# Pooled attention and two expert layers on one core: the maximum of the scores is subtracted by TensorE in PSUM, and ScalarE copies the router logits

## The chip, the cores and the metric

The kernel runs on one core of a Trainium2 chip. The metric is the device time of one execution in microseconds; lower is better. TensorE has two clock levels, 1.2 and 2.4 GHz, and the profile shows the granted share of the full clock for every stretch.

## The reference, cut to what matters

Three stages follow one another. Keys and values are averaged over groups of eight rows, so that each of the 576 queries of a head sees 72 pooled keys. The softmax subtracts the row maximum before the exponential. Two expert layers (router, then the product with the chosen expert's weights) come after it.

```python
k_p = k.reshape(B, H, Sp, pool, D).mean(axis=3)
v_p = v.reshape(B, H, Sp, pool, D).mean(axis=3)
scores = scale * np.matmul(q, k_p.transpose(0, 1, 3, 2))
scores = scores - np.max(scores, axis=-1, keepdims=True)
attn = np.exp(scores)
attn = attn / (np.sum(attn, axis=-1, keepdims=True) + 1e-09)
return np.matmul(attn, v_p)          # then _moe_ref and _moe2_ref
```

B = H = 8, S = 576, D = 64, pool = 8, so Sp = 72.

## The kernel before

The attention works through 36 chunks `c` of 128 tokens, all eight heads at once. Each chunk is a chain over four engines, and the chain is spread over several turns of one loop, so that every engine has work of several chunks in its queue. Every engine executes its queue in the order in which the code was written.

In one turn of the loop, for chunk `c`, these steps are issued:

- `emit_S(c)`: TensorE multiplies the transposed queries `qt` with the pooled keys `KB` into `ps_s` (two banks of PSUM; there is one such buffer, so the next chunk's product waits until the last reader is done). Inside it stands `emit_qT(c + 2)`, four transposes of queries and their copy `qt` by ScalarE. VectorE reduces `ps_s` to the eight maxima `mx`, then subtracts them into `ec` in SBUF; ScalarE takes the exponential of `ec` in place.
- `emit_eT(c - 1)`: TensorE transposes the exponentials of the chunk before into `ps_et`, ScalarE copies them to `et`.
- `emit_AV(c - 3)`: TensorE multiplies `et` with `VB` (pooled values, a column of ones and the values times the router's weights) into `ps_av`. VectorE makes `rec` (two operations), `lg` and the attention output `x` out of it. The rest of that chunk, the sum `ls`, the logits `LG` and the copy of the logits into the last eight columns of `x`, is issued in the next turn, around the maximum and the subtraction of chunk `c + 1`.
- `prep_...` and `pool_...`: the sums over eight rows (on GpSimd, and a third of the values on VectorE, the instruction `v<-v` of line 172) and their transposes and copies for later batches. `VB<-v,half` and `VB<-ps_g,half` are VectorE's part of the values' preparation.
- `bg.tick()`: one small step of a background chain (routing of finished tokens), at fixed places between these.

Of every nine chunks one holds the last 64 tokens of two batches; its products are done in two halves of 64 rows. I call it a mixed chunk. The first block of the first expert layer starts between the last chunks (`moe.gemm1_early`), and everything after the attention follows from there, mostly at the pace of TensorE.

The lines that the change and the prediction's steps touch are these, with the numbers of the profile: 293 (product of the scores), 303 (`mx`), 307 (subtraction), 309 (exponential), 327 and 329 (`et`), 347 (product with the values), 366 to 382 (what VectorE does with it), 172, 247 and 259 (pooling and preparation on VectorE).

Of the kernel before, what the change touches and what calls it, by code (L numbers as in the profile page):

```python
# [19 lines left out]
POOL = 8  # L20
# [14 lines left out]
# Tiles of pooled rows of K: four, from the third batch on.  # L35
# [3 lines left out]
# Pooled rows (head, sp) of one batch: five tiles for K, six chunks for V.  # L39
# [4 lines left out]
def segments(t):  # L44
    """Pieces of a tile of pooled rows that belong to one batch: (b, sp0, sp1, first partition)."""
    g0, end = TILES[t]
    g = g0
    while g < end:
        b, sp = divmod(g, SP)
        n = min(SP - sp, end - g)  # L50
        yield b, sp, sp + n, g - g0
        g += n


def attention(tc, g, q, k, v, mid, w_gate, bias, const, moe):
    """Pooled attention; rows of (x, router logits) go to g.xd in token order, logits to g.LG.

    The first block of the first layer starts while the last tokens are still at work."""
    nc = tc.nc
    with ExitStack() as ctx:  # L60
# [46 lines left out]
        def load_kb(b, i0, i1):  # L107
            """Pooled rows (head, sp) of K of one batch, tiles i0 to i1."""
            if ("kb", b) not in raw_t:
                raw_t["kb", b] = raw.tile([128, 5, POOL * D], F32, tag="k", name="kb", bufs=3)  # L110
            a = raw_t["kb", b]
            n = KR[i0][1] - KR[i0][0]
            nc.sync.dma_start(out=a[0:n, i0:i1, :],
                              in_=rows(k, b, KR[i0][0], KR[i1 - 1][1], i1 - i0))
# [53 lines left out]
        def pool_rows(out, a, eng):  # L168
            """Sums over the rows of a pool: a [n, m, POOL * D] to out [n, m, D]."""
            n, m = a.shape[0], a.shape[1]  # L170
            if eng is nc.vector:
                eng.tensor_reduce(out=out, in_=a.rearrange("p h (r d) -> p h d r", r=POOL),
                                  axis=AX.X, op=ALU.add)
            else:
                t1 = tree.tile([128, 4, 4 * D], F32, tag="t1", name="t1")[0:n, 0:m]
                t2 = tree.tile([128, 4, 2 * D], F32, tag="t2", name="t2")[0:n, 0:m]
                eng.tensor_tensor(t1, a[:, :, 0:4 * D], a[:, :, 4 * D:], ALU.add)
                eng.tensor_tensor(t2, t1[:, :, 0:2 * D], t1[:, :, 2 * D:], ALU.add)
                eng.tensor_tensor(out, t2[:, :, 0:D], t2[:, :, D:], ALU.add)
# [19 lines left out]
        def prep_kb(b, eng=None):  # L199
            """Even heads to the upper half of the partitions, odd ones to the lower."""  # L200
# [9 lines left out]
            # the last head in the place of the first, which the lower half doesn't need  # L210
# [77 lines left out]
        def emit_S(c, then=lambda: None):  # L288
            t = qT.pop(c)
            ps = ps_s.tile([128, 2, 512], F32, tag="s", name="ps_s")  # L290
            for b, p0, p1 in parts(c):
                for hp in range(4):
                    nc.tensor.matmul(ps[p0:p1, hp // 2, (hp % 2) * 144:(hp % 2) * 144 + 144],
                                     lhsT=t[:, hp, p0:p1], rhs=KB[b % NR][:, hp, :],
                                     start=True, stop=True)
# [3 lines left out]
            mx = sm.tile([128, 2, 4], F32, tag="mx", name="mx")  # L299
            ec = ep.tile([128, 2, 4, SP], F32, tag="ec", name="ec", bufs=2)  # L300
            e = ec.rearrange("p g h s -> p (g h s)")
# [5 lines left out]
            nc.vector.tensor_tensor(ec, view, mx.unsqueeze(3).to_broadcast([128, 2, 4, SP]),  # L307
                                    ALU.subtract)
            nc.scalar.activation(out=e, in_=e, func=ACTF.Exp, scale=1.0 / (POOL * 8.0))
            bg.tick()  # L310
# [3 lines left out]
            e_t[c] = e  # L314
# [43 lines left out]
        def after_AV(c, ps):  # L358
# [23 lines left out]
            V.tensor_copy(x[:, r, DM:XW], g.LG[:, c, :])  # L382
# [41 lines left out]
        # loads in the order of their use  # L424
# [27 lines left out]
        # the part of a chunk's rows that belongs to its first and to its second head  # L452
# [10 lines left out]
        # the clock of the tensor engine rises while nothing has come yet  # L463
# [10 lines left out]
        emit_S(0, lambda: emit_qT(1))  # L474
        for j in range(6):
            h = 4 * (j // 3) + j % 3
            i = 64 * (j % 2)
            nc.scalar.copy(WGV[i:i + 64, j // 2, j % 2].rearrange("p (a e) -> p a e", a=2),
                           wg[i:i + 64, h:h + 2, :])
        pool_v(0, 0, nc.vector)  # L480

        def bias_table():
            """The bias of every token: (1 - m) * b0 + m * b1."""
# [40 lines left out]
        for c in range(NC + LAG):  # L524
# [8 lines left out]
            elif c < 4:  # L533
                if c > 0:
                    emit_S(c)
                    emit_eT(c - 1)
                emit_qT(c + 2)
            elif c == NC - 1:
                emit_S(c, moe.gemm1_early)
            if 4 <= c < NC:  # L540
                emit_eT(c - 1)
            if c == NC - 1:
# [73 lines left out]
class Late:  # L616
    """The pool of the time of use."""
# [5 lines left out]
class Background:  # L623
    """Chains of small steps, spread between the steps of the main work."""
# [18 lines left out]
    def settle(self):  # L643
        """Until no product of theirs waits to be read."""
# [8 lines left out]
def setup(tc, g, const):  # L653
# [4 lines left out]
                            pattern=[[-1, 128]], channel_multiplier=1)  # L658
    g.LG = const.tile([128, C1, E], F32, name="LG")
# [12 lines left out]
def setup_routing(tc, g, const):  # L672
    """Constants and tables of both layers' routing."""
# [9 lines left out]
    # -1 where the row isn't before the column  # L683
# [49 lines left out]
    # the token of every column and partition, plus one, in two parts  # L733
# [44 lines left out]
def route(tc, g, r, lg, mask, c0, n, sp, pp, eng, wait=1, then=()):  # L778
    """The expert of every token of n columns, and its place among the expert's tokens, in steps."""
# [103 lines left out]
def together(*gens):  # L883
    """Steps of several chains in turn."""
# [10 lines left out]
def early_pick(tc, g, r, sp, pp, wait=4, fill=None):  # L895
    """The expert with the most tokens so far: its tokens come first."""
# [33 lines left out]
def keep_places(tc, g, r, n, f, sp):  # L930
    """Where fewer than n tokens of the first expert are known, the places up to n stay empty."""
# [14 lines left out]
def early_places(tc, g, r, C, j0, n, sp):  # L946
    """Which of the first C columns' tokens have one of n columns of places from j0 on."""
# [17 lines left out]
def early_slots(tc, g, r, C, gidx, sp, pp, empty=None):  # L965
    """The tokens of these places."""
# [33 lines left out]
def route_counts(tc, g, r, sp, pp, wait=1):  # L1000
    """Blocks of every expert; those of the first expert come first."""
# [33 lines left out]
def route_blocks(tc, g, r, sp):  # L1035
    """Every block's expert, and whether it isn't that of the block before."""
# [12 lines left out]
    # the tokens up to the end of a block's expert, less 256 for every block before  # L1049
# [26 lines left out]
def route_slots(tc, g, r, sp, pp, pace=1):  # L1076
    """The token of every slot."""
# [41 lines left out]
class Moe:  # L1119
    """The two expert layers, in blocks of T tokens of one expert."""  # L1120
# [91 lines left out]
    def zero(self):  # L1212
        """Nothing has a place in these columns before the eighteenth block."""
# [147 lines left out]
    def run(self):  # L1361
# [6 lines left out]
        # layer 1  # L1368
# [28 lines left out]
        # layer 2  # L1397
# [3 lines left out]
    def start2(self):  # L1401
        """Layer 2's first expert, and the tokens of its first two blocks, from 16 blocks of layer 1."""
# [13 lines left out]
    def gather_next(self, i):  # L1416
        """Block 0 of layer 2 in the place of block i of layer 1, if that doesn't exist."""
# [5 lines left out]
    def first2(self, n):  # L1423
        """Block 0 of layer 2, after n blocks of layer 1."""
# [36 lines left out]
    def deferred1(self, i, eng):  # L1461
        """Layer 2's gates of block i of layer 1, in steps."""
# [76 lines left out]
class Layer:  # L1539
    """Blocks of one layer, each prepared while the one before is computed."""  # L1540
# [22 lines left out]
    def second(self):  # L1563
        """Block 1, of the same expert as block 0; the places of the later ones are still at work."""
# [185 lines left out]
```

## Time and profile before

| | |
|---|---|
| time, median of 3 runs | 1028.99 us (1028.85 to 1032.23) |
| span of the profiled execution, first to last instruction | 1021.7 us |
| what lies around the span, against the median | 7.3 us |
| TensorE matmuls busy | 953.3 us (93%) |
| VectorE busy | 713.9 us (70%) |
| ScalarE busy | 526.0 us (51%) |
| GpSimd busy | 606.4 us (59%) |

The shares are means over the span. The attention is its first fifth (the maxima of the 36 chunks lie between 12.5 and 204.4 us), and the shares of that stretch are others than those of the expert layers, so they are read from the stretch. Engines are named PE (TensorE's matmuls), PEld (its weight loads), DVE (VectorE), ACT (ScalarE), POOL (GpSimd) and SP. An operation's row gives its start, its duration and, in brackets, how long its engine was idle before it and what ended the idle time.

### The profile page before, as it was taken

Reading aid. Unit: us, or ns where it says so; the run is one execution under the profiler, and the core shown is the slowest. Engines: PE = TensorE matmul, PEld = TensorE weight load, DVE = VectorE, ACT = ScalarE, POOL = GpSimd, SP = SyncE. Lnnn points to the kernel's source line nnn. Section 1 sums busy time; section 2 is a strip of 40 time slices with the busy share of each in tenths; the row PEclk is TensorE's granted clock in tenths of the full one; section 3 lists DMA queues with packets and bytes.
Section 4 is the critical chain, followed back from the end, with each engine's and each line's share of the span. In section 5 each row is a group of like instructions: output and inputs, shape, how many; then the busy total and the mean of one; then the engine's idle time right before and its main releaser. Section 6 shows DMA issues by size and latency. Waiting matters only on the chain. (4 is left out here: it accounts for less than half of the span.)

```text
span 1021.7 us, 20008 instructions
## 1 busy us (share of the span) xinstructions
PE 953.3 (93%) x6647; PEld 859.1 (84%) x6647; DVE 713.9 (70%) x1683; ACT 526.0 (51%) x1072; POOL 606.4 (59%) x816
## 2 busy tenths in 40 slices
PE   6888879899999999999999999999898999999995
PEld 5787879787788888888888888888786998888995
DVE  6699998886666666666666766667455667667665
ACT  4345545432455555555555655555313556555454
POOL 4675856554577777677777777767544333444442
PEclk8789989998999999999999999999899999999998
DMA  9998864520111111342223511226214662661341
GB/s 226 205 248 245 199 172 156 177 68 9 43 53 68 56 60 57 126 148 69 71 73 118 170 68 62 70 71 206 93 56 132 217 226 83 204 207 33 103 154 31
DMA packets 88353, 123.51 MB, mean 121 GB/s; under 512 B 15615, under 2 KB 52479, under 8 KB 88224
## 3 DMA queue, kind: packets, MB, share of 16 engines
q1 hardware_dynamic: 77904, 94.38, 30.9%
q0 software_dynamic: 10320, 27.59, 8.6%
q8 instruction: 59, 0.97, 0.4%
q14 instruction: 70, 0.57, 0.2%
HBM read 181.29 MB, written 39.48 MB: 216 GB/s over the span
## 5 line engine op out<-in xcount | busy, mean ns | idle before, releaser
L1300 PE MATMUL ps_g<-xh,w1h 128*128 128x256 f32 x992 | 289.2, 291 | 13.2 <-DVE hl L1304 8.0
L1300 PE MATMUL ps_g<-xl,w1h 128*128 128x256 f32 x992 | 280.2, 283 | 0.0
L1300 PE MATMUL ps_g<-xh,w1l 128*128 128x256 f32 x992 | 280.2, 282 | 0.0
L1253 POOL TENSOR_TENSOR w1l<-w1r,w1h 128x512 fp32r<-128x512 f32 x122 | 156.6, 1305 | 150.9 <-ACT w1h L1252 150.1
L1303 ACT ACTIVATE hh<-ps_g 128x256 fp32r<-128x256 f32 x248 | 95.5, 385 | 231.4 <-PE ps_g L1300 225.8
L1300 PEld LDWEIGHTS ps_g<-xh,w1h 128*128 128x128 f32 x992 | 188.2, 190 | 22.1 <-DVE hl L1304 10.5
L1314 PE MATMUL ps_g<-w2h,hh 128*128 128x512 f32 x464 | 190.5, 411 | 0.6 <-DVE rs_v L994 0.5
L1300 PEld LDWEIGHTS ps_g<-xl,w1h 128*128 128x128 f32 x992 | 188.6, 190 | 0.6 <-DVE xl L1269 0.2
L1300 PEld LDWEIGHTS ps_g<-xh,w1l 128*128 128x128 f32 x992 | 188.2, 190 | 0.0
L1314 PE MATMUL ps_g<-w2h,hl 128*128 128x512 f32 x464 | 185.1, 399 | 0.0
L1314 PE MATMUL ps_g<-w2l,hh 128*128 128x512 f32 x464 | 185.0, 399 | 0.0
L1259 DVE TENSOR_TENSOR w2l<-w2r,w2h 128x512 fp32r<-128x512 f32 x227 | 162.9, 719 | 17.7 <-ACT w2h L1258 1.5
L1304 DVE SCALAR_TENSOR_TENSOR hl<-ps_g,hh 128x256 fp32r<-128x256 f32 x248 | 105.0, 423 | 91.4 <-ACT hh L1303 85.9
L1258 ACT CAST w2h<-w2r 128x512 fp32r<-128x512 f32 x232 | 141.8, 612 | 3.0 <-DVE gidxf L997 3.0
L1252 ACT CAST w1h<-w1r 128x512 fp32r<-128x512 f32 x240 | 135.4, 618 | 4.9 <-DMA w1r<-in_moe_w_dram 4.9
L859 POOL TENSOR_SCALAR OB<-iota,BB,pay 128x128 bf16<-128x128 bf16 x126 | 110.8, 888 | 24.7 <-DVE BB L847 24.7
L1314 PEld LDWEIGHTS ps_g<-w2h,hl 128*128 128x128 f32 x464 | 88.3, 190 | 20.8
L1253 DVE TENSOR_TENSOR w1l<-w1r,w1h 128x512 fp32r<-128x512 f32 x118 | 101.2, 880 | 5.6 <-POOL rt_eq L796 5.2
L1314 PEld LDWEIGHTS ps_g<-w2h,hh 128*128 128x128 f32 x464 | 88.5, 191 | 18.1 <-issue 1.5
L1314 PEld LDWEIGHTS ps_g<-w2l,hh 128*128 128x128 f32 x464 | 88.6, 191 | 16.8
L1269 DVE TENSOR_TENSOR xl<-ps_x,xh 128x512 fp32r<-128x512 f32 x64 | 43.8, 686 | 57.3 <-ACT xh L1268 57.3
L1373 ACT ACTIVATE x<-ps_g,gate 128x512 f32<-128x512 f32 x37 | 25.5, 689 | 82.4 <-PE R L831 43.4
(256 smaller groups left out, 1463.9 us busy)
## 6 DMA issues: line engine op xcount, KB each, us to landing
w1r<-in_moe_w_dram SPq DMA_DIRECT2D x128, 512.0 KB
w2r<-in_moe_w_dram SPq DMA_DIRECT2D x128, 512.0 KB
x2s<-x SPq DMA_DIRECT2D x19, 522.0 KB
v<-in_v_dram SPq DMA_DIRECT2D x16, 576.0 KB
xd<-x SPq DMA_DIRECT2D x16, 520.0 KB
q_sb<-in_q_dram SPq DMA_DIRECT2D x16, 512.0 KB
kt<-in_k_dram SPq DMA_DIRECT2D x8, 576.0 KB
x2s<-OBx SPq DMA_DIRECT2D x16, 261.0 KB
```

Source lines behind the costliest of these rows:

```text
L859: e.tensor_scalar(g.ob(c)[:, i, :], g.iota, r.BB[:, c:c + 1], r.pay[:, i, c:c + 1], ALU.is_equal, ALU.mult)
L1252: self.nc.scalar.copy(self.w1h[f], raw)
L1253: (eng or self.nc.vector).tensor_tensor(self.w1l[f], raw, self.w1h[f].bitcast(F32), ALU.subtract)
L1258: self.nc.scalar.copy(self.w2h[f], raw)
L1259: (eng or self.nc.vector).tensor_tensor(self.w2l[f], raw, self.w2h[f].bitcast(F32), ALU.subtract)
L1269: nc.vector.tensor_tensor(self.xl[i % 2][:, :, 128 * t:128 * t + 128], ps, hi.bitcast(F32), ALU.subtract)
L1300: nc.tensor.matmul(ps, lhsT=a[f][:, k, :], rhs=b[:, k, :], start=(n == 0), stop=(n == 11))
L1303: nc.scalar.activation(out=self.hh[f], in_=ps, func=ACTF.Relu)
L1304: nc.vector.scalar_tensor_tensor(self.hl[f], in0=ps, scalar=0.0, in1=self.hh[f].bitcast(F32), op0=ALU.max, op1=ALU.subtract)
L1314: nc.tensor.matmul(ps, lhsT=a[f][:, tt], rhs=b[f], start=(n == 0), stop=(n == 23))
L1373: nc.scalar.activation(out=self.x2[i % 2][:, t, 0:DM], in_=ps, func=ACTF.Copy, scale=self.gate[i % 2][:, t:t + 1])
```

## The change

The subtraction leaves VectorE. VectorE writes the maxima `mx` in a type that TensorE reads in one pass (`F32R`, rounded). TensorE then adds minus the identity times `mx`, each maximum repeated over the 72 keys of its head, onto the scores where they lie in PSUM: two matmuls of 288 columns for each chunk. ScalarE takes the exponential straight from PSUM and writes `ec`. These two steps are a new function, `emit_exp(c)`, called after `emit_eT(c - 1)`. The product of the scores changes its start and stop flags, so that the later matmuls add to it. The copy of the logits into `x` goes from VectorE to ScalarE. Minus the identity, `nident`, is made once by GpSimd.

```diff
                     nc.tensor.matmul(ps[p0:p1, hp // 2, (hp % 2) * 144:(hp % 2) * 144 + 144],
                                      lhsT=t[:, hp, p0:p1], rhs=KB[b % NR][:, hp, :],
-                                     start=True, stop=True)
+                                     start=(hp % 2 == 0), stop=(hp % 2 == 1),
+                                     skip_group_check=True)
...
-            mx = sm.tile([128, 2, 4], F32, tag="mx", name="mx")
-            ec = ep.tile([128, 2, 4, SP], F32, tag="ec", name="ec", bufs=2)
-            e = ec.rearrange("p g h s -> p (g h s)")
+            mx = sm.tile([128, 2, 4], F32R, tag="mx", name="mx")
             next(av)
             nc.vector.tensor_reduce(out=mx, in_=view, axis=AX.X, op=ALU.max)
             bg.tick()
             next(av)
             bg.tick()
-            nc.vector.tensor_tensor(ec, view, mx.unsqueeze(3).to_broadcast([128, 2, 4, SP]),
-                                    ALU.subtract)
-            nc.scalar.activation(out=e, in_=e, func=ACTF.Exp, scale=1.0 / (POOL * 8.0))
-            bg.tick()
+            s_t[c] = ps, mx
             for _ in av:
                 pass
             bg.tick()
-            e_t[c] = e
+
+        s_t = {}
+
+        def emit_exp(c):
+            ps, mx = s_t.pop(c)
+            for gg in range(2):
+                nc.tensor.matmul(ps[:, gg, 0:288], lhsT=g.nident,
+                                 rhs=mx[:, gg, :].unsqueeze(2).to_broadcast([128, 4, SP]),
+                                 start=False, stop=True, skip_group_check=True)
+            e = e_t[c] = ep.tile([128, 8 * SP], F32, tag="ec", name="ec", bufs=2)
+            nc.scalar.activation(out=e.rearrange("p (g n) -> p g n", g=2), in_=ps[:, :, 0:288],
+                                 func=ACTF.Exp, scale=1.0 / (POOL * 8.0))
+            bg.tick()
...
-            V.tensor_copy(x[:, r, DM:XW], g.LG[:, c, :])
+            nc.scalar.copy(x[:, r, DM:XW], g.LG[:, c, :])
...
             if 4 <= c < NC:
                 emit_eT(c - 1)
+                emit_exp(c)
...
+    g.nident = const.tile([128, 128], F32R, name="nident")
+    nc.gpsimd.tensor_scalar(g.nident, g.ident, -1.0, None, ALU.mult)
```

The order of the queues shows where the new work stands. TensorE's queue before, one chunk without preparation and the start of the next (`ps_s` is the scores, `ps_q` the transposed queries, `ps_et` the transposed exponentials, `ps_av` the product with the values, three chunks back):

```order
L293 MATMUL ps_s<-KB_126,qt 128x144 x4
L272 MATMUL ps_q<-ident,qs 128x128 x4
L327 MATMUL ps_et<-ident,ec 96x128 x6
L347 MATMUL ps_av<-VB_132,et 128x146 x6
L293 MATMUL ps_s<-KB_127,qt 128x144 x4
```

The same place of the changed kernel:

```order
L293 MATMUL ps_s<-KB_128,qt 128x144 x4
L272 MATMUL ps_q<-ident,qs 128x128 x4
L336 MATMUL ps_et<-ident,ec 96x128 x6
L317 MATMUL ps_s<-mx,nident 128x288 x2
L356 MATMUL ps_av<-VB_134,et 128x146 x6
L293 MATMUL ps_s<-KB_129,qt 128x144 x4
```

The two new matmuls, which read the maxima `mx` of this chunk, stand ahead of the product with the values.

VectorE's queue before, from the maximum of one chunk to that of the next (`rec`, `lg` and `x` read the product with the values, `v<-v` is the pooling of values):

```order
L303 TENSOR_REDUCE mx<-ps_s 128x8
L380 TENSOR_TENSOR LG<-ls,BT 128x8
L307 TENSOR_TENSOR ec<-ps_s,mx 128x576
L382 COPY x<-LG 128x8
L366 TENSOR_SCALAR rec<-ps_av 128x8
L368 RECIPROCAL rec<-rec 128x8
L371 TENSOR_TENSOR lg<-ps_av,rec 128x64
L373 TENSOR_TENSOR x<-ps_av,rec 128x512
L172 TENSOR_REDUCE v<-v 96x64
L378 TENSOR_REDUCE ls<-lg 128x8
L303 TENSOR_REDUCE mx<-ps_s 128x8
```

The same stretch of the changed kernel:

```order
L302 TENSOR_REDUCE mx<-ps_s 128x8
L389 TENSOR_TENSOR LG<-ls,BT 128x8
L375 TENSOR_SCALAR rec<-ps_av 128x8
L377 RECIPROCAL rec<-rec 128x8
L380 TENSOR_TENSOR lg<-ps_av,rec 128x64
L382 TENSOR_TENSOR x<-ps_av,rec 128x512
L172 TENSOR_REDUCE v<-v 96x64
L387 TENSOR_REDUCE ls<-lg 128x8
L302 TENSOR_REDUCE mx<-ps_s 128x8
```

The subtraction and the copy are gone from between `LG` and `rec`; the rest stands as it stood.

ScalarE's queue before, one chunk (`qt` and `qs` are queries of later chunks, `vt` is a part of the values' preparation):

```order
L276 COPY qt<-ps_q 128x512
L309 ACTIVATE ec<-ec 128x576
L329 COPY et<-ps_et 96x768
L163 COPY qs<-q_sb 128x1024
L246 COPY vt<-ps_v 128x288
```

The same of the changed kernel:

```order
L276 COPY qt<-ps_q 128x512
L391 COPY x<-LG 128x8
L338 COPY et<-ps_et 96x768
L321 ACTIVATE ec<-ps_s 128x576
L163 COPY qs<-q_sb 128x1024
L246 COPY vt<-ps_v 128x288
```

The copy of the logits stands ahead of the copy `et`, and the exponential of this chunk has moved behind that copy.

## Rows read from the trace of the kernel before

**Rows 1.** The page: span and busy time of each engine.

```profile
span 1021.7 us, 20008 instructions
...
PE 953.3 (93%) x6647; PEld 859.1 (84%) x6647; DVE 713.9 (70%) x1683; ACT 526.0 (51%) x1072; POOL 606.4 (59%) x816
```

**Rows 2.** Busy time of each engine in two stretches of 20 us: PE, PEld, DVE, ACT and POOL, each with its count; then the granted clock, the DMA share and GB/s.

```profile
100.00:120.00 20.00, 19.26 (x162) 18.35 (x160) 19.68 (x52) 11.81 (x21) 13.90 (x15) 1.00 0.64 168
...
160.00:180.00 20.00, 20.00 (x200) 19.59 (x199) 15.35 (x47) 12.96 (x20) 9.34 (x11) 1.00 0.59 183
```

**Rows 3.** Groups of instructions by line in the first 260 us, shapes kept apart: count, busy us, mean ns of one, idle time of the engine before them and what ended it.

```profile
L329 ACT COPY et<-ps_et 96x768 f32<-96x768 f32 x36 | 28.0, 778 | 1.9 <-PE ps_et L327 1.9
L307 DVE TENSOR_TENSOR ec<-ps_s,mx 128x576 f32<-128x576 f32 x36 | 27.1, 753 | 0.7
...
L309 ACT ACTIVATE ec<-ec 128x576 f32<-128x576 f32 x36 | 24.6, 684 | 72.6 <-DVE ec L307 69.9 <-DVE x L382 2.6
...
L380 DVE TENSOR_TENSOR LG<-ls,BT 128x8 f32<-128x8 f32 x36 | 16.6, 462 | 0.1
...
L382 DVE COPY x<-LG 128x8 f32<-128x8 f32 x36 | 13.7, 380 | 0.1
...
L478 ACT COPY WGV<-wg 64x16 f32<-64x16 f32 x6 | 1.2, 203 | 1.6 <-DMA wg<-in_moe_w_gate_dram 1.6
```

**Rows 4.** VectorE in order of time, from the maximum of chunk 7 to that of chunk 8: start, duration, instruction.

```profile
57.87 0.74 DVE L303 TENSOR_REDUCE mx<-ps_s 128x8 f32<-128x576 f32 x1
58.53 0.15 DVE L380 TENSOR_TENSOR LG<-ls,BT 128x8 f32<-128x8 f32 x1
58.71 0.76 DVE L307 TENSOR_TENSOR ec<-ps_s,mx 128x576 f32<-128x576 f32 x1
59.38 0.16 DVE L382 COPY x<-LG 128x8 f32<-128x8 f32 x1
59.45 0.16 DVE L366 TENSOR_SCALAR rec<-ps_av 128x8 f32<-128x8 f32 x1
...
60.63 1.06 DVE L172 TENSOR_REDUCE v<-v 96x64 f32<-96x512 f32 x1
61.61 0.26 DVE L378 TENSOR_REDUCE ls<-lg 128x8 f32<-128x64 f32 x1
61.78 0.75 DVE L303 TENSOR_REDUCE mx<-ps_s 128x8 f32<-128x576 f32 x1
```

**Rows 5.** All engines in order of time around the end of chunk 12's subtraction: what TensorE starts when it is done.

```profile
86.54 0.75 DVE L307 TENSOR_TENSOR ec<-ps_s,mx 128x576 f32<-128x576 f32 x1
...
87.40 1.03 PEld L293 LDWEIGHTS ps_s<-KB,qt 128*128 128x128 f32 x8 [0.74 <-issue]
87.43 1.22 PE L293 MATMUL ps_s<-KB,qt 128*128 128x144 f32 x8 [0.55 <-DVE ec L307]
...
88.49 0.60 PE L272 MATMUL ps_q<-ident,qs 128*128 128x128 f32 x4
...
88.92 0.82 PE L327 MATMUL ps_et<-ident,ec 128*96 128x128 f32 x6
```

**Rows 6.** Products with the values: one of a plain chunk with VectorE's first operation after it, which had waited for it, and one of a mixed chunk.

```profile
160.47 1.66 PE L347 MATMUL ps_av<-VB,et 96*128 96x146 f32 x12
...
162.17 0.17 DVE L366 TENSOR_SCALAR rec<-ps_av 128x8 f32<-128x8 f32 x1 [1.02 <-PE ps_av L347]
...
172.09 2.77 PE L347 MATMUL ps_av<-VB,et 96*64 96x146 f32 x24
```

**Rows 7.** Two matmuls in a row of the type `F32R`, 256 columns each, in the first block of the first expert layer.

```profile
201.35 0.28 PE L1300 MATMUL ps_g<-xh,w1l 128*128 128x256 f32 x1
201.47 0.28 PE L1300 MATMUL ps_g<-xh,w1h 128*128 128x256 f32 x1
```

**Rows 8.** Stretches bounded by the maxima of chunks 0, 5, 27 and 35, each answer narrowed to one line: VectorE's busy us with the count, granted clock, DMA share, GB/s. First line 303 in the three stretches, then, for the stretch from chunk 5 to chunk 27, lines 172, 247 (with POOL's share behind VectorE's), 259, 380 and 382.

```profile
12.00:45.70 33.70, 3.76 (x5) 0.75 0.97 203
45.70:164.30 118.60, 16.39 (x22) 0.94 0.80 212
164.30:203.60 39.30, 5.98 (x8) 1.00 0.51 170
...
45.70:164.30 118.60, 18.92 (x18) 0.94 0.80 212
...
45.70:164.30 118.60, 5.00 (x5) 2.94 (x2) 0.94 0.80 212
...
45.70:164.30 118.60, 1.46 (x6) 0.94 0.80 212
...
45.70:164.30 118.60, 14.14 (x22) 0.94 0.80 212
...
45.70:164.30 118.60, 9.60 (x22) 0.94 0.80 212
```

**Rows 9.** One long `LG` of VectorE, and what GpSimd did meanwhile.

```profile
62.45 3.18 DVE L380 TENSOR_TENSOR LG<-ls,BT 128x8 f32<-128x8 f32 x1
...
63.26 2.34 POOL L177 TENSOR_TENSOR t<-kt 108x1024 f32<-108x1024 f32 x1
```

**Rows 10.** Near the end of the attention, where tokens of the first expert block are transposed between two chunks: the product with the values of chunk 29, and the maximum of chunk 33.

```profile
187.76 1.73 PE L347 MATMUL ps_av<-VB,et 96*128 96x146 f32 x12
...
192.54 0.74 DVE L303 TENSOR_REDUCE mx<-ps_s 128x8 f32<-128x576 f32 x1
```

More of the change, by code (lines that the diff above doesn't have):

```diff
@@ L474, in attention @@
         emit_S(0, lambda: emit_qT(1))
+        emit_exp(0)
         for j in range(6):
@@ L541, in attention @@
                 emit_eT(c - 1)
+                emit_exp(c)
             if c == NC - 1:
```

## Prediction

> **What bounds the kernel now.** I read the page first: TensorE is busy 93% of the span and VectorE 70% [rows 1]. These are means over two different stages. The change touches only the attention, so I turned to the busy time by stretch: around 100 to 120 us VectorE is busy 19.68 of 20 us and TensorE 19.26; around 160 to 180 us TensorE fills all 20 and VectorE 15.35 [rows 2]. So the attention is bound by VectorE while VectorE also pools values, and by TensorE after that. What comes later follows at TensorE's pace, so I take it that a shift of the attention's end moves the end of the kernel by as much.
>
> Then the pace. Between the maxima of chunks 5 and 27 lie 22 chunks in 118.6 us, 5.39 us each; the next eight take 39.3 us, 4.91 each [rows 8]. One chunk of VectorE without disturbance is 3.91 us from maximum to maximum [rows 4]. The rest is held operations (`LG` takes 0.15 us alone but 0.46 on average, the copy of the logits 0.16 against 0.38 [rows 3, 4]), steps of preparation and routing, and waits. A long `LG` ends when GpSimd's operation ends [rows 9]: 62.45 + 3.18 = 65.63, and 63.26 + 2.34 = 65.60.
>
> **What is removed.** From VectorE, 36 subtractions, 27.1 us, and 36 copies, 13.7 us [rows 3]. That is 40.8 us, and read as a saving it would be 4%. Whether it is one depends on what VectorE waits for afterwards.
>
> **What is added, and the new loop.** In TensorE's queue the two matmuls that read `mx` stand ahead of the product with the values of three chunks earlier. TensorE starts in order: in [rows 5] it idles 0.55 us for the subtraction in front of the product of the scores, and the transposes behind that product, which read another tile, come only after it. So in the changed kernel the product with the values waits for this chunk's maximum. VectorE's `rec`, `lg` and `x` wait for that product, and in VectorE's queue the next maximum stands behind them. This closes a loop through both engines, which no buffer opens. Its length:
>
> - the maximum, 0.74 us [rows 4];
> - the hand-over from VectorE to TensorE, 0.14: the subtraction ends at 87.29, the product starts at 87.43 [rows 5];
> - the two new matmuls. None like them is in the trace. Matmuls of the same type and 256 columns follow each other every 0.12 us [rows 7], so 288 columns take some 0.13, two 0.27; I take 0.30 to the start of what follows. The upper bound is the price of the scores' type: eight records of 144 columns take 1.06 us [rows 5], 0.13 each and two for one product, so 288 columns twice are 1.06. I take the lower, since the type is that of [rows 7];
> - the product with the values, 1.66, and 0.04 until `rec` starts [rows 6];
> - from `rec` to the next maximum, 2.33 with a pooling operation, of which that operation is 0.98, so 1.35 without [rows 4].
>
> Together 4.23 us without and 5.21 with pooling. Before, the same plain chunk took 3.91 with pooling: there the product with the values ran beside the maximum and the subtraction.
>
> A rule of the Trainium skill ("TensorE: Matmul & The Clock Gate", Part 3, The mechanism) says that matmuls start and end in program order but that weight loads may be pulled ahead. By its second half the load of `nident` would be done during the wait. In [rows 5] the load starts at 87.40, after the wait, and the matmul 0.03 later. By the rule the hand-over would be some 0.1 shorter, 3 us over all chunks; by the row it is not, and I go by the row.
>
> **The stretch from chunk 5 to 27.** 22 x 4.23 = 93.1. Eighteen pooling operations at 0.98 add 17.6; five `VB<-v,half` (5.00 us in all, about 0.95 each without overlap) 4.8; six `VB<-ps_g,half` at 0.17 1.0 [rows 8]; two mixed products at 2.77 instead of 1.66 [rows 6] 2.2. That is a floor of 118.7 us, where before all of it took 118.6. Three more terms come on top.
>
> - Background steps. Before, 22 x 2.93 = 64.5 without pooling, the same 17.6, 4.8 and 1.0, and the held time, 14.14 - 22 x 0.15 = 10.8 for `LG` and 9.60 - 22 x 0.16 = 6.1 for the copy [rows 8], make 104.8; the other 13.8 us are background steps and waits. Four of the six places for such steps lie between the maximum and `rec`, which is now waiting time; two lie in the loop: a third, 4.6.
> - The clock. The stretch was granted 0.94 [rows 8], and TensorE's part of the loop, 1.96 us, now counts in it: 6% of 22 x 1.96 is 2.6, and nothing if the shorter gaps keep the clock up. I take 1.4.
> - Held `LG`. ScalarE's queue is now: copy of the logits, `et`, exponential. From the start of the maximum to the next one over this path: 0.81 until `LG` is done, 0.27 for the hand-over and the copy (0.20, the nearest copy of that size), 0.78 for `et`, 0.68 for the exponential [rows 3], 0.14, 1.22 for the next scores, 0.04: 3.94. That leaves cover of 0.29 us in a plain chunk and 1.27 with pooling. The 10.8 us of held `LG` come in pieces up to 3 us [rows 9]; spread evenly they cost nothing, in five such pieces about 5. I take 2. The copy's held 6.1 us vanish with it, since ScalarE does it now.
>
> Sum 126.7, which is 8.1 us more than before.
>
> **The rest.** In the next eight chunks TensorE had 1.06 + 0.43 + 0.65 + 1.49 = 3.63 us of work per plain chunk (starts and, for the last two, durations less the tail of 0.17 that the next group overlaps [rows 5, 6]). The loop of 4.23 binds there: 0.6 us each for five chunks, 3.0. In about three chunks the first expert block's tokens stand between the product with the values and the next maximum, 4.78 us from one to the other [rows 10]; that path now starts 0.74 + 0.14 + 0.30 = 1.18 later, 3.5 in all. One of the eight is paced by VectorE's routing steps and gets 0.75 back. After the last maximum the product of chunk 32 is late by at most 1.18; I take 0.8. Together 6.5.
>
> The first five chunks take 33.7 us with the DMA engines 0.97 busy [rows 8]; their bound is transfers, and I add 0.5 (nothing to 5 x 0.3). `nident` is one operation of GpSimd, once: nothing.
>
> **Sum.** 0.5 + 8.1 + 6.5 = 15.1 us. The profiled span is 1021.7, so 1036.8 there; what lies around the span, 7.3 us, stays, and the time is 1028.99 + 15 = 1044 us. The three runs lie 0.3% apart, so I call 0.5%, 5.1 us, the least that counts as a difference.
>
> **Rivals.**
>
> - *VectorE's saving counts in full.* If the maximum were done before TensorE reached the new matmuls, VectorE's own work would set the pace: 118.6 - 22 x 0.75 - 6.1 = 96.0, 23 less, and with 5 lost in the TensorE-bound part the time is 1011. For it: VectorE is busy 98% of [rows 2]'s first stretch. Against it: the loop has to shrink by 0.9 us per pooling chunk, and every part of it is a duration or a start in a row. It decides where the maximum ends before the transposes of the exponentials do.
> - *A draw.* Only the floor of 118.7 is met in the stretch, the held time having bought the loop, and the tail loses 3 us because the maxima come earlier: 1029 to 1035, centre 1032. For it: 16.9 us of held time in 22 chunks. Against it: background steps do not vanish.
> - *The new matmuls are dear.* At the upper bound they take 1.06 instead of 0.30, 0.76 more in some 31 loops, 23.6: 1067; half of that 1056. For it: their moving operand repeats one value 72 times, and no row shows such a read. Against it: nothing in the rows makes one column dearer than another.
>
> **How the numbers follow.** The forecast, 1036 to 1052, gets 0.65 (its own bounds: `LG` -2 to +3, clock -1.4 to +1.2, background steps and tail 3 either way). The draw 0.15, the full saving 0.08, the dear matmuls 0.12. The range 1030 to 1056 leaves out the full saving and the worse half of the dear matmuls, some 0.15 in all. Faster by over 0.5%: 0.08 and a little of the draw, 0.09. Slower: 0.65 + 0.12 and the draw's end above 1034.1, 0.78. Within 0.5%: 0.13.
>
> **What would show each step.** In the changed profile TensorE should idle in front of the new matmuls, released by `mx`, and VectorE in front of `rec`, released by `ps_av`, in most chunks; the busy share of VectorE in the attention should fall to about 75% without the chunks coming faster; a pooling chunk should take about 5.2 us and a plain one about 4.2 from maximum to maximum. The two new matmuls should start 0.12 to 0.15 us apart. I am wrong if the product with the values starts before the maximum of its turn ends, if the 22 chunks take under 115 us, or if later stages take up the delay.

## The result, and the profile after

The changed kernel takes 1038.83 us in the median (1037.33 to 1042.64, four runs), beside 1028.92 of the kernel before: a ratio of 1.0125, 95% interval 1.0092 to 1.0157. In a second comparison it was 1.0118 (1.0060 to 1.0175). It is slower, by more than the 0.5% that I had called the least that counts. The forecast was 1044, range 1030 to 1056.

The page of the changed kernel, as [rows 1]: span and busy times.

```profile
span 1037.6 us, 20084 instructions
...
PE 961.8 (93%) x6719; PEld 865.4 (83%) x6719; DVE 680.0 (66%) x1611; ACT 529.8 (51%) x1108; POOL 606.3 (58%) x817
```

VectorE has 34 us less work, and the span is 15.9 us longer. The same two stretches as in [rows 2]:

```profile
100.00:120.00 20.00, 16.82 (x139) 15.55 (x138) 15.04 (x46) 9.99 (x19) 5.89 (x6) 1.00 0.53 144
160.00:180.00 20.00, 17.73 (x150) 16.82 (x150) 12.57 (x45) 11.28 (x22) 13.56 (x17) 1.00 0.56 173
```

VectorE (third) falls from 19.68 to 15.04 and TensorE (first) from 19.26 to 16.82: neither engine is full. What they wait for stands in the groups by line in the first 265 us (busy us, mean ns, then idle time and what ended it):

```profile
L317 PE MATMUL ps_s<-mx,nident 128*128 128x288 f32 x72 | 19.4, 354 | 29.4 <-DVE mx L302 29.3
L375 DVE TENSOR_SCALAR rec<-ps_av 128x8 f32<-128x8 f32 x36 | 6.0, 165 | 57.2 <-PE ps_av L356 57.1
L321 ACT ACTIVATE ec<-ps_s 128x576 f32<-128x576 f32 x36 | 23.3, 648 | 0.4 <-PE ps_s L317 0.4
L389 DVE TENSOR_TENSOR LG<-ls,BT 128x8 f32<-128x8 f32 x36 | 16.7, 463 | 0.1
L391 ACT COPY x<-LG 128x8 f32<-128x8 f32 x36 | 7.1, 198 | 48.7 <-DVE LG L389 48.7
```

TensorE waits for `mx` in front of the new matmuls and VectorE waits for `ps_av` in front of `rec`: the two halves of the loop. One turn of it without disturbance, chunk 28, in order of time:

```profile
184.93 0.75 DVE L302 TENSOR_REDUCE mx<-ps_s 128x8 fp32r<-128x576 f32 x1
...
185.73 0.30 PEld L317 LDWEIGHTS ps_s<-mx,nident 128*128 128x128 f32 x2
185.74 0.51 PE L317 MATMUL ps_s<-mx,nident 128*128 128x288 f32 x2
...
186.09 1.66 PE L356 MATMUL ps_av<-VB,et 96*128 96x146 f32 x12
...
187.78 0.17 DVE L375 TENSOR_SCALAR rec<-ps_av 128x8 f32<-128x8 f32 x1 [2.03 <-PE ps_av L356]
...
188.36 0.68 DVE L382 TENSOR_TENSOR x<-ps_av,rec 128x512 f32<-128x512 f32 x1
...
189.14 0.75 DVE L302 TENSOR_REDUCE mx<-ps_s 128x8 fp32r<-128x576 f32 x1
```

From maximum to maximum 4.21 us, predicted 4.23: 0.75, hand-over 0.06 (predicted 0.14), 0.35 from the first new matmul to the product (predicted 0.30), 1.66, 0.03, and 1.36 to the next maximum. With one pooling operation, chunks 10, 15 and 21 take 5.19, 5.17 and 5.16, predicted 5.21.

The stretches between the maxima of chunks 0, 5, 27 and 35, narrowed to the maxima, as in [rows 8]:

```profile
12.30:44.80 32.50, 3.73 (x5) 0.84 0.95 198
44.80:180.50 135.70, 16.41 (x22) 0.95 0.74 192
180.50:224.50 44.00, 5.99 (x8) 0.96 0.41 135
```

The 22 chunks took 135.7 us, before 118.6, predicted 126.7. The last eight took 44.0, before 39.3. After the last maximum the changed kernel needed 813.0 us, 5 less than the 818.0 of before. Most of these 5 come back at one place, the border between the expert layers. Here are all engines' busy times from one transposition of tokens to the end of that border, first of before, then of the changed kernel:

```profile
709.45:745.40 35.95, 31.34 (x182) 27.70 (x180) 17.63 (x38) 14.13 (x30) 20.24 (x31) 0.91 0.39 126
```

```profile
730.60:762.10 31.50, 28.79 (x184) 25.18 (x182) 16.81 (x39) 14.05 (x30) 21.06 (x31) 1.00 0.43 140
```

Before, TensorE stood still there twice, 1.80 and 2.04 us, and the stretch was granted 0.91; in the changed kernel it stood once and kept the clock. In brackets the idle time ("issue": it waited for nothing that the profile shows), the second of before and the one of after:

```profile
722.50 0.58 PE L1300 MATMUL ps_g<-xh,w1h 128*128 128x256 f32 x1 [2.04 <-issue]
```

```profile
741.31 0.36 PE L1314 MATMUL ps_g<-xh,w1h 128*128 128x256 f32 x1 [1.97 <-issue]
```

I know no reason why the change should do that. Whether it is the chance of one execution, the first experiment asks.

### The profile page after: what moved, and what is told of

Same layout as the page of the kernel before. It is cut to its first block, busy times and chain, and to the rows that moved or that the text cites. A ratio compares the mean times of both kernels' runs of the same rounds, so it can differ in the third digit from the quotient of the medians.

```text
span 1037.6 us, 20084 instructions
## 1 busy us (share of the span) xinstructions
PE 961.8 (93%) x6719; PEld 865.4 (83%) x6719; DVE 680.0 (66%) x1611; ACT 529.8 (51%) x1108; POOL 606.3 (58%) x817
```

## The experiments

Times are medians, with the kernel before run on the same chip beside them (1027.5, 1026.6 and 1027.0 us in the three groups). All kernels have the 36 chunks; "6 to 27" is the time from the maximum of chunk 6 to that of chunk 27.

**The kernel before, unchanged.**

> The kernel before once more, unchanged, for a second profile. The two profiles at hand differ by 15.9 us of span, but the maximum of chunk 35 comes 20.9 us later in the changed kernel; 4.9 us are given back at one place, between the two expert layers. If that is chance of a single execution, this span is some 5 us longer than the 1021.7 us of the first profile, the maximum of chunk 35 again near 203.7 us, and the difference lies behind 714 us. If the gain belongs to the change, this profile repeats the first one: 1021 to 1023 us.

Its span was 1020.2, its own time 1022.05. So 1.85 us lie around a span. The 7.3 us that I took for it were mostly an execution of before that was 5 us faster than the median.

The border repeats itself too. Here is TensorE's busy time from the first routing matmul `R` at the border to the transposition `ps_lt`, in the two profiles of before and then in the two of the changed kernel (the clock is the third number from the right):

```profile
717.49:733.74 16.25, 12.40 (x79) 0.79 0.18 58
717.92:733.50 15.58, 12.03 (x80) 0.78 0.20 55
739.12:750.44 11.32, 9.35 (x79) 1.00 0.20 53
745.26:755.99 10.73, 9.71 (x80) 1.00 0.21 52
```

In all four profiles of kernels whose subtraction stays on VectorE this stretch takes 13.1 to 16.3 us, at 0.78 to 0.87 of the full clock; in all ten with the subtraction on TensorE it takes 10.2 to 12.7 us at 1.00. So the shorter border is not chance, it goes with the change; why, no run shows. The later layers as a whole are not always shorter: after the last maximum the second profiles need 814.4 us (before) and 814.3 (changed).

**The loop opened.** In the changed kernel `emit_exp(c)` is issued behind the product with the values.

```diff
             if 4 <= c < NC:
                 emit_eT(c - 1)
-                emit_exp(c)
...
             emit_AV(c - LAG)
+            if 4 <= c < NC:
+                emit_exp(c)
```

> The changed kernel with one step moved: the new matmuls and the exponential are issued behind the product with the values of three chunks earlier, not ahead of it. All work is the same. Loop theory: the product no longer waits for the maximum, VectorE no longer waits for it in front of rec, and the pace becomes that of the ring scores, transposes, product, new matmuls, exponential, scores on TensorE and ScalarE, about 4.8 us per plain chunk: 22 chunks in about 108 us instead of 135.7, the tail of eight chunks in about 41, the time near 1015 to 1022 us, faster than both kernels. Rival, that the new matmuls or ScalarE's longer queue themselves cost the time: no more than 3 us change, 1036 to 1040 us.

1031.86 us, ratio 1.0039 (1.0016 to 1.0061): 7 of the 10 us come back, by nothing but this order. "6 to 27" falls from 127.7 to 119.2. I had expected 1015 to 1022 us. One part of what is missing is chunk 5, which takes 14.4 us instead of 7.9, since VectorE waits 9.5 us there for a load of values. Another is a second loop that shows now. The turn of chunk 27 to 28 in this kernel:

```profile
182.75 0.51 PE L317 MATMUL ps_s<-mx,nident 128*128 128x288 f32 x2
...
183.35 0.65 ACT L321 ACTIVATE ec<-ps_s 128x576 f32<-128x576 f32 x1 [1.01 <-PE ps_s L317]
...
184.05 1.25 PE L293 MATMUL ps_s<-KB,qt 128*128 128x144 f32 x8 [0.80 <-ACT ec L321]
...
185.34 0.76 DVE L302 TENSOR_REDUCE mx<-ps_s 128x8 fp32r<-128x576 f32 x1 [0.86 <-PE ps_s L293]
```

The next scores need the one buffer `ps_s`, whose last reader is now the exponential, and TensorE idles 0.80 us for it; its waits between 56 and 176 us:

```profile
PE ps_s L293 <- ACT ec L321: 15.8, 20, 2.4
```

In the changed kernel the product with the values stands in this place and covers that wait; before, the reader was VectorE's subtraction, which comes earlier.

**The pair doubled.** Minus half the identity, two pairs of matmuls.

```diff
-            for gg in range(2):
+            for gg in (0, 1, 0, 1):
...
-    nc.gpsimd.tensor_scalar(g.nident, g.ident, -1.0, None, ALU.mult)
+    nc.gpsimd.tensor_scalar(g.nident, g.ident, -0.5, None, ALU.mult)
```

> The changed kernel with minus half the identity and the pair of new matmuls issued twice, so the sum taken from the scores is the same. It doubles the price of the new matmuls and moves nothing else. Loop theory (TensorE's wait for the maximum, the pair and the product with the values lie in one loop that sets every chunk from the fifth on): the pair takes about 0.25 to 0.35 us from its start to that of the product with the values in the changed kernel's trace, so about 0.25 to 0.35 us more in each of some 31 loops, 8 to 11 us, less the chunks that something else paces: 1045 to 1050 us against the 1039 of the changed kernel, and plain chunk 28 about 4.5 us instead of 4.2. Rival (the new matmuls are off the path, and the exponential or the held additions set the pace): 1038 to 1041.

1049.09 us (1.0239, 1.0203 to 1.0274). Chunk 28 in this kernel:

```profile
192.14 0.76 DVE L302 TENSOR_REDUCE mx<-ps_s 128x8 fp32r<-128x576 f32 x1
...
192.95 0.76 PE L317 MATMUL ps_s<-mx,nident 128*128 128x288 f32 x4
...
193.55 1.66 PE L356 MATMUL ps_av<-VB,et 96*128 96x146 f32 x12
...
196.60 0.74 DVE L302 TENSOR_REDUCE mx<-ps_s 128x8 fp32r<-128x576 f32 x1
```

0.60 us from the first new matmul to the product instead of 0.35, and 4.46 from maximum to maximum instead of 4.21: what is put into the loop comes out of it whole, and the pair costs 0.25. From the maximum of chunk 6 to that of chunk 35, 29 chunks, the profile is 7.1 us longer. The dear matmuls (0.76 more each turn) are out.

**The halves of the change.** Before, with only the copy of the logits moved; and the changed kernel, with the copy back on VectorE.

```diff
-            V.tensor_copy(x[:, r, DM:XW], g.LG[:, c, :])
+            nc.scalar.copy(x[:, r, DM:XW], g.LG[:, c, :])
```

> The kernel before with one part of the change alone: the copy of the logits goes to ScalarE, the subtraction stays on VectorE. VectorE sets the pace there, so it should gain the copy with its held time: 6 us of held time and 22 x 0.08 in the stretch from chunk 5 to 27, a little in the tail, so 1020 to 1024 us. If the held time only moves on to LG or VB, which share the port with GpSimd, it stays within 2 us of before.

> The changed kernel with the copy of the logits back on VectorE: the subtraction alone is moved. Loop theory: VectorE waits some 2 us between the maximum and rec, the copy lies in that wait, so giving it back costs nothing to 2 us: 1037 to 1041 us. If VectorE's busy time counted, the copy's 13.7 us of the trace before would come back and the time would be near 1048 us.

The copy alone: 1028.74 us, 1.0018 (0.9995 to 1.0041), no gain where I had expected 4 to 8 us. VectorE loses 13.7 us of copies, `LG` falls to 14.0, the copy on ScalarE costs 0.18 each:

```profile
L380 DVE TENSOR_TENSOR LG<-ls,BT 128x8 f32<-128x8 f32 x36 | 14.0, 388 | 0.1
...
L382 ACT COPY x<-LG 128x8 f32<-128x8 f32 x36 | 6.6, 182 | 5.9 <-DVE LG L380 5.9
```

Yet "6 to 27" is 113.9 against 111.7 and 114.1 in the two profiles of before. The time that a copy was held is not gained when it leaves VectorE. It did not move on to `LG` either, which is shorter too. The stretch ran at 0.93 of the full clock instead of 0.95, with one stop of TensorE of 7.3 us between the maxima of chunks 21 and 23, so this profile leaves open what took the time.

The subtraction alone: 1051.02 us, 1.0199 (1.0156 to 1.0242), worse than with the copy on ScalarE, and not the 1037 to 1041 us that I had expected; the rival's 1048 is nearer. But chunk 28 takes 4.22 us here as in the changed kernel, so the copy does not lengthen the loop. Its "6 to 27" is 135.0 us at a granted clock of 0.87, where the changed kernel has 127.7 at 0.95. The next runs show where that comes from.

**The copy behind the exponential.** The changed kernel; ScalarE copies the logits after the exponential, so that a held `LG` holds up neither `et` nor the exponential. Then both kernels side by side.

```diff
-            s_t[c] = ps, mx
-            for _ in av:
-                pass
+            next(av)
+            s_t[c] = ps, mx, av
...
                                  func=ACTF.Exp, scale=1.0 / (POOL * 8.0))
+            for _ in av:
+                pass
...
             yield
+            yield
             nc.scalar.copy(x[:, r, DM:XW], g.LG[:, c, :])
```

> The changed kernel with ScalarE's copy of the logits issued behind the exponential instead of ahead of the copy et. It takes one thing away: a held LG no longer holds the copy et and the exponential behind it in ScalarE's queue, and with them the next scores. Theory (the term that I sized at 2 us was too small because of these pieces): the chunks with a held LG of 3 us (the eighth and the twelfth or so) get shorter by about 0.8 to 1.8 us each, smaller pieces by less, 3 to 5 us in all: 1034 to 1036 us. Rival (VectorE's own queue behind the held LG sets these chunks, ScalarE doesn't matter): no change, 1038 to 1040, with the chunks of a held LG as long as in the changed kernel.

> The changed kernel itself, unchanged, on the same chip as the next run. It says how much of the stretch from chunk 6 to chunk 27 is fixed and how much goes with the granted clock: the first profile of it took 127.8 us there at 0.95, and two variants that keep the loop took 135 us at 0.86 and 0.87. Theory (the clock falls in this kernel by chance, execution by execution, and each twentieth of it costs some 4 us): times between 1036 and 1046 us, and the stretch of the new profile at its clock on that line. Rival (the changed kernel keeps 0.95 and the variants lose the clock for a reason of their own): 127 to 129 us at 0.95 again.

> ScalarE's copy of the logits behind the exponential, the same kernel as before, now beside the changed kernel on one chip. Theory (a held LG through ScalarE's queue costs some 3 us in all, and its first run was hidden by a lower clock of the stretch): 1 to 4 us under the run beside it, and at an equal clock a stretch shorter by about 3 us. Rival (the held LG costs nothing beyond VectorE's own queue): the same as the run beside it within 1 us at an equal clock.

1043.40 us (1.0156, 1.0117 to 1.0195) and again 1043.78 (1.0179, 1.0132 to 1.0225), beside 1042.46 of the changed kernel (1.0118, 1.0060 to 1.0175): no gain where I had expected 3 to 5 us, perhaps a loss. What it aimed at happened all the same. A held `LG` in the changed kernel, chunk 8:

```profile
66.32 3.19 DVE L389 TENSOR_TENSOR LG<-ls,BT 128x8 f32<-128x8 f32 x1
...
67.13 2.34 POOL L177 TENSOR_TENSOR t<-kt 108x1024 f32<-108x1024 f32 x1
...
69.53 0.20 ACT L391 COPY x<-LG 128x8 f32<-128x8 f32 x1 [2.98 <-DVE LG L389]
...
69.64 0.79 ACT L338 COPY et<-ps_et 96x768 f32<-96x768 f32 x1
...
70.33 0.65 ACT L321 ACTIVATE ec<-ps_s 128x576 f32<-128x576 f32 x1
...
71.03 1.53 PE L293 MATMUL ps_s<-KB,qt 128*128 128x144 f32 x8 [2.31 <-ACT ec L321]
...
72.59 0.76 DVE L302 TENSOR_REDUCE mx<-ps_s 128x8 fp32r<-128x576 f32 x1 [1.75 <-PE ps_s L293]
```

`LG` ends at 69.51, GpSimd's operation at 69.47; then ScalarE's queue runs off in order, and VectorE waits 1.75 us for the scores. With the copy behind the exponential this chunk takes 5.1 us instead of 6.9. From maximum to maximum in us, with the granted clock of the chunk in brackets:

| chunk | changed | changed again | copy behind | copy behind again | copy on VectorE |
|---|---|---|---|---|---|
| 8 | 6.9 (0.95) | 7.3 (0.90) | 5.1 (1.00) | 5.1 (1.00) | 5.3 (1.00) |
| 12 | 6.6 (1.00) | 6.6 (1.00) | 5.1 (1.00) | 5.0 (1.00) | 5.2 (1.00) |
| 13 | 6.1 (1.00) | 6.2 (1.00) | 7.7 (0.99) | 7.4 (1.00) | 7.6 (1.00) |
| 14 | 5.3 (1.00) | 5.4 (1.00) | 7.5 (0.50) | 7.0 (0.60) | 7.5 (0.52) |
| 20 | 6.5 (1.00) | 6.6 (1.00) | 10.0 (0.54) | 8.8 (0.63) | 8.7 (0.63) |
| 6 to 27 | 127.7 (0.95) | 126.6 (0.95) | 134.6 (0.86) | 130.6 (0.90) | 135.0 (0.87) |

Chunk 12 comes earlier, and in chunk 13 GpSimd's next operation meets VectorE's routing steps instead. The copy behind the exponential, chunk 13 to the start of 14:

```profile
97.79 2.35 POOL L177 TENSOR_TENSOR t<-kt 108x1024 f32<-108x1024 f32 x1
97.88 2.35 DVE L808 TENSOR_TENSOR rt_eq<-LG,rt_mx 128x72 f32<-128x72 f32 x1
...
100.27 1.28 DVE L810 TENSOR_SCALAR rt_eq<-rt_eq 128x72 f32<-128x72 f32 x1
...
104.68 0.74 DVE L302 TENSOR_REDUCE mx<-ps_s 128x8 fp32r<-128x576 f32 x1
...
105.48 0.61 PE L316 MATMUL ps_s<-mx,nident 128*128 128x288 f32 x1 [3.35 <-DVE mx L302]
```

The routing step, 0.23 us where nothing holds it, takes 2.35; `rec` and the next maximum come late; TensorE waits 3.35 us for `mx`. In the same chunk of the second profile the next routing step is held, and with the copy on VectorE it is `LG`:

```profile
96.40 2.24 DVE L810 TENSOR_SCALAR rt_eq<-rt_eq 128x72 f32<-128x72 f32 x1
```

```profile
102.63 2.21 DVE L389 TENSOR_TENSOR LG<-ls,BT 128x8 f32<-128x8 f32 x1
```

TensorE's waits for `mx` behind them are 3.00 and 3.20 us. Then the clock falls. Chunks 13 and 14 of the copy behind the exponential, first profile, by busy time (TensorE first; the clock is the third number from the right):

```profile
96.97:104.68 7.71, 4.36 (x35) 4.11 (x35) 7.64 (x16) 3.18 (x6) 5.10 (x5) 0.99 1.01 239
104.68:112.17 7.49, 6.69 (x29) 6.68 (x30) 4.10 (x15) 1.68 (x3) 0.00 (x0) 0.50 0.25 90
```

Chunk 14 runs at the lower level and takes 7.5 us instead of 5.3. The copy on VectorE likewise frees ScalarE's queue, and has the same pattern. So my theory of chance falls: the changed kernel kept 0.95 twice, the variants were at 0.86 to 0.90 three times, and they lose it at the same place. The held time moved on, and behind the wait that it made in the loop the clock fell. That the wait is the cause is read from the order of events; no run takes it away by itself. The opposite case is there too: in the second profile of the copy behind the exponential, chunk 6 begins with such a wait and then takes 5.3 us at 1.00:

```profile
54.32 0.51 PE L316 MATMUL ps_s<-mx,nident 128*128 128x288 f32 x2 [3.35 <-DVE mx L302]
```

**A new order.** Scores, product with the values, new matmuls, transposes of the exponentials, transposes of the queries; first alone, then with the copy behind the exponential.

```diff
-                emit_S(c, lambda: emit_qT(c + 2))
+                emit_S(c)
...
-            if 4 <= c < NC:
+            if c == NC - 1:
                 emit_eT(c - 1)
                 emit_exp(c)
...
             emit_AV(c - LAG)
+            if 4 <= c < NC - 1:
+                emit_exp(c)
+                emit_eT(c - 1)
+                emit_qT(c + 2)
```

> The changed kernel with TensorE's order of a turn made new: scores, product with the values of three chunks back, the new matmuls, the transposes of the exponentials of the chunk before, the transposes of the queries. The product now covers the maximum, and the two groups of transposes cover the exponential, so neither loop should leave TensorE idle: 1.06 + 1.49 + 0.30 + 0.65 + 0.43 = 3.9 us of TensorE's work per plain chunk, where the run with only the product moved ahead had 4.9 us in its last plain chunks. Theory (what that run still lost was TensorE's wait for the exponential, 15.8 us of waits between chunks 6 and 27): 1020 to 1027 us, faster than before. Rival (what it still lost is held LG and late transfers, which the order doesn't touch): 1028 to 1033.

> The new order of the run before and ScalarE's copy of the logits behind the exponential, together. Theory: a held LG then delays neither the exponential nor the next scores; 2 to 4 us less than the new order alone, 1017 to 1024 us, faster than before. Rival (late transfers and VectorE's own queue set what is left): the same as the new order alone within 2 us.

1025.51 us (0.9984, 0.9962 to 1.0006) and 1025.09 (0.9983, 0.9960 to 1.0007). The whole loss is gone and the new order is level with before, not faster as I had expected; the copy's place adds nothing that can be measured, where I had expected 2 to 4 us. Chunk 28 takes 3.8 us in both, as TensorE's work said (3.9). In the second one, VectorE's largest wait between 40 and 215 us is now a transfer:

```profile
DVE v L172 <- DMA v<-in_v_dram: 13.9, 2, 8.3
```

**The pooling of values later**, for the two batches whose load was waited for; in the last kernel, and in the kernel before.

```diff
-        for b, c0 in ((1, 3), (2, 5), (3, 9), (4, 13), (5, 16), (6, 18), (7, 21)):
+        for b, c0 in ((1, 3), (2, 7), (3, 9), (4, 13), (5, 16), (6, 18), (7, 23)):
...
-                pool_at.setdefault(c0 + min(i, 1) if b == 1 else c0 + i, []).append((pool_v, b, 1, V, i, i + 1))
+                pool_at.setdefault(c0 + min(i, 1) if b <= 2 else c0 + i, []).append((pool_v, b, 1, V, i, i + 1))
...
-                   8: [(prep_v1, 2, P)], 9: [(prep_v2, 2)],
+                   9: [(prep_v1, 2, P)], 10: [(prep_v2, 2)],
```

> The new order of TensorE's queue and the copy behind the exponential, and VectorE's share of the pooling of values issued one or two chunks later for two batches (the third and the eighth), whose load VectorE waited for by 8.3 and 5.5 us in that run. Theory (the waits for these two loads now set the attention's pace): up to 13.8 us less than that run, some of it given to other waits: 1012 to 1020 us, faster than both kernels. Rival (the loads, not the place of their reader, set the pace, since the next loads wait for the buffers that are now read later): 1021 to 1028.

> The kernel before with nothing but the same pooling of values issued later. It says how much of the run above the later pooling gives by itself. Before, VectorE waited for these loads only 0.3 us, so 1025 to 1030, no change. Rival (before too is paced by these loads, hidden in other waits): 1018 to 1023.

1025.05 us (0.9978, 0.9957 to 0.9999) and 1022.31 (0.9957, 0.9936 to 0.9978): both in the range of the rival, not of what I had expected. In the first, chunk 6 comes at 47.4 us instead of 55.0, and the wait moves on to the next batch, in chunk 9:

```profile
77.73 1.02 DVE L172 TENSOR_REDUCE v<-v 96x64 f32<-96x512 f32 x1 [10.45 <-DMA v<-in_v_dram]
```

So the loads set the pace there, not the place of their reader. The kernel before with this one edit is the fastest of all, by 0.4%, which is under my 0.5% but outside the noise. Its profile doesn't show why: its last maximum of the attention is at 204.8 us, 203.7 and 205.9 in the two of before, whose executions were faster than their median. That stays open.

## Why the prediction was right, and where its sum was not

Right: slower, within the range, and for the reason given. The forecast of +15 us is more than the +9.9 between the medians of the first comparison and near the +15.4 of the second. The loop is there, its length is right to 0.02 us in chunk 28 and to 0.05 in undisturbed chunks with pooling, opening it takes back most of the loss, and lengthening it lengthens the chunks by as much. The stages, between the profiles:

| | predicted | measured |
|---|---|---|
| up to the maximum of chunk 5 | +0.5 | -0.9 |
| chunks 5 to 27 | +8.1 | +17.1 |
| chunks 27 to 35 and what follows at once | +6.5 | +4.7 |
| later layers | 0 | -5.0 |
| span | +15.1 | +15.9 |

The sum came out by errors that cancel, and that is luck: it has 9.0 us too little between chunks 5 and 27, and 1.4, 1.8 and 5.0 too much in the three other stages.

- *The term held `LG` was sized at 2 us.* Counting every chunk against the loop (4.21, 0.98 for each pooling operation, 0.95 and 0.17 for the steps of `VB`, 1.1 for a mixed product), 17.4 us are left over in the 22 chunks where I had 8.0. Chunks 8, 12 and 19, with `LG` at 3.19, 3.11 and 1.88, have 5.5 of them. I had the path through ScalarE right and its cover of 0.29 too, but spread the pieces: two of them fell into chunks without pooling, at the least cover.
- *Other held steps had no term.* `VB<-v,half` takes 2.07 instead of 0.95 in chunk 16, routing and token steps 1.0 to 1.25 in chunks 9 and 13. With a transfer 1.4 us late in chunk 5, these four chunks have 5.9; chunk 9 ran at 0.82 of the clock, so a part of its 2.1 belongs to the next point. The background steps without a hold, chunks 22 to 26, have 2.2; I had 4.6 for all.
- *The clock was sized at 1.4.* Chunks 6, 7 and 17, at 0.65 to 0.82, have 3.8; the first two take just the loop's 5.3 and 5.2 us at full clock in the second run with the copy behind the exponential, and the last does in the changed kernel's second profile.
- *That a shift of the attention passes to the end* was wrong by 5 us of 21 in the first profiles, though I had named this as a sign of being wrong. Most of it is the border of the expert layers, which is shorter with the change for a reason that stays open. Between the second profiles the shift passes whole, 22.9 us at the last maximum and at the end.
- *"What lies around the span, 7.3 us, stays"* was wrong. It is 1.85, and the rest was a quick execution of before, whose span I set beside a median: 1021.7 + 1.85 + 15.9 is 1039.4, the own time of the changed kernel's profile, and the 1044 were 5 us too many.

The smaller terms: the hand-over is 0.06. That is shorter, as I had drawn from the Trainium skill ("TensorE: Matmul & The Clock Gate", Part 3, The mechanism), but not by its rule: the row shows the load of `nident` at 185.73, behind the maximum's end at 185.68, so nothing was pulled ahead. The section says it under a condition that I had left out (a load for other row groups, or into the background weight buffer); no run here shows whether it holds for this load. In chunk 29, where the engine had to wait for the maximum, the load starts 0.05 behind the maximum's end at 189.89, with its matmul:

```profile
189.94 0.30 PEld L317 LDWEIGHTS ps_s<-mx,nident 128*128 128x128 f32 x2 [0.37 <-DVE mx L302]
189.94 0.51 PE L317 MATMUL ps_s<-mx,nident 128*128 128x288 f32 x2
```

What it saved, the pair took: its matmuls start 0.23 apart, not 0.12 to 0.15. VectorE's saving did not count: the loop never shrank under VectorE's own work.

## What to carry to other kernels

Work that is taken off the busiest engine is worth nothing when the engine that takes it stands in front of what the first one waits for: follow the queues once round before adding up savings. Look then for an order in which each wait is covered by other work of the same engine; here that alone was worth some 13 us. And count operations that another engine holds as a cost of the schedule, which can move to the next operation when the order of work shifts: look at the chunk behind the one that got shorter.

## What the runs showed of the hardware

A stop of TensorE of 3.00 to 3.35 us at the start of chunk 14 was followed by 0.50 to 0.60 of the full clock over that chunk in all three profiles of two variants, and the chunk took some 2 us more each time; I had treated the clock as a few per cent on everything. It is not so after every such stop, as chunk 6 with 3.35 us and 1.00 shows.

GpSimd held VectorE's operations on several kinds: `LG`, routing steps, `VB`. `x<-ps_av,rec`, with one input in PSUM, took 680 to 682 ns in all 25 instances between 40 and 190 us. The Trainium skill ("SBUF — State Buffer", SBUF: two separate sides) says that the port pair which the two engines share is locked for a whole instruction, where VectorE's operation has two inputs in SBUF or runs in a mode that uses both ports; the trace agrees, with `LG` at 0.15 us alone and 3.19 when held to GpSimd's end.

A moving operand that repeats each value 72 times costs TensorE nothing that shows: the second pair of matmuls of 288 columns of `F32R` adds 0.25 us, where the 0.12 us for 256 columns of [rows 7] would give 0.27. ScalarE's exponential is faster from PSUM, 648 ns, than in place in SBUF, 684 ns [rows 3].
